# Down projection of channels 0 to 511 with tokens on the accumulators' partitions, and the last block stored by token groups from two queues

## The chip, the cores and the metric

The kernel runs on one core of a Trainium2 chip. The core has five engines with instruction streams of their own: TensorE (PE) multiplies matrices and writes only to PSUM, VectorE (DVE) and ScalarE (ACT) work element by element and read and write PSUM and SBUF, GpSimd (POOL) works on SBUF, and SyncE (SP) issues transfers between the chip's memory and SBUF. ACT can issue transfers too. A weight load (PEld) puts the stationary operand of a product into the array, 128 rows by up to 128 columns; then the other operand, 128 rows by up to 512 columns, moves through. The product has the stationary operand's columns on its partitions. The metric is the device time of one launch in microseconds (us), as the median of several runs.

## What is computed

One transformer-like block for 2048 tokens with 640 channels. A conditioning vector `c` gives six rows of 640 (`sa, ca, ga, sb, cb, gb`). The first half is a layer norm and a long convolution over the tokens (by Fourier transforms); the second half, where the change lies, is a gated feed-forward layer:

```python
h = _layernorm(x) * (1 + cb) + sb
gate = einsum("bsd,df->bsf", h, w1)      # 640 -> 1728
up   = einsum("bsd,df->bsf", h, w3)      # 640 -> 1728
out  = einsum("bsf,fd->bsd", silu(gate) * up, w2)   # 1728 -> 640, the down projection
x = x + gb * out
```

## The kernel before

**Tiling.** The 2048 tokens are four blocks (b = 0 to 3) of 512. In `x2[b]` a block lies with 128 tokens on the partitions, four token groups j beside each other and 640 channels each, so `x2[b][p, j, d]`. The hidden width 1728 is cut into 14 tiles m: thirteen of 128 and one (m = 13) of 64, which is stacked twice to fill 128 rows. The 640 channels of the output are five groups k of 128.

**Precision.** Every operand is split into a high and a low part (`split`, L595: ACT copies the high part, DVE subtracts for the low one), and a product is made of three: high by high, high by low, low by high.

**The passes.** `ffn` (L1344) runs two passes, p = 0 for blocks 0 and 1, p = 1 for blocks 2 and 3. In a pass, `groups` (L1355) goes through the hidden tiles and makes gate and up for both blocks by a seven-product scheme (`group`, L828, and `last_group`, L882); the hidden values of the first block of the pair go straight into the down projection (`mid`, L1366, calls `down` for the tile before), those of the second block are kept in SBUF as `h`. Then `late` (L1387) finishes the first block's accumulators, adds them to `x2` and stores them, while the down projection of the second block runs over the 14 kept tiles in the order `H` (13, 0, 1, ..., 12). In `late(0)` the layer norm of blocks 2 and 3 is interleaved as well, and after the loop `plain` makes tile 13 of blocks 2 and 3 (the `gh` products) before the second pass begins.

**The down projection.** `down` (L964) adds tile m to the five accumulators `acc[k]`, one PSUM bank of 512 columns each: channels on the partitions, the block's 512 tokens on the columns. A slice of w2 of 128 channels is stationary and the hidden values (`ah`, `al`) move. Per tile these are 15 products (10 for m = 13, whose low part lies in the stacked rows).

**Out of the accumulators.** `gated` (L974) copies `acc[k]` to SBUF on ACT and scales it by the gate of its channel, which is a number for each partition (`cols[:, 2, k]`). `output` (L979) turns the 128 x 512 tile back with four PE transposes into one bank, and DVE adds the bank to channels k of `x2[b]`. `store` (L987) writes `x2[b]` to the output, one transfer for each quarter q of the partitions.

**Banks and buffers.** Five of the eight PSUM banks are the accumulators; the other three rotate under the tag `gu` for everything else: the products of gate and up, the transposes of `output`, and those of the layer norm. w2 tiles rotate through three SBUF buffers (tag `w2`, 640 KB each); in `late`, tile i + 2 is asked for in iteration i (L1444), into the buffer that tile i - 1 leaves.

**Order.** PE's instructions in this part follow the order of the program text (the wrapper `InOrder`, L142, through which `self.pe` is called; its line L151 is the one that the profile names). The streams of the other engines and of SP are laid out in a fixed order before the launch; each engine then works through its own in order and waits on semaphores. In `late`, the list `extra` says after which iteration which piece of other work is put: the outputs of k = 0 after iteration 0, k = 1 and 2 after 1, k = 3 and 4 after 2, and the stores of the quarters after 3, 5, 7 and 9. The second block's last two tiles are kept back in `late(1)` (`LAST = 2`) and done group by group (L1451 to L1461), so that group k can be scaled, turned, added and stored while group k + 1 is multiplied: channels 0 to 383 in four transfers after k = 3, the remaining 256 channels in four more, two from SP and two from ACT.

Of the kernel before, what the change touches and what calls it, by code (L numbers as in the profile page):

```python
# [10 lines left out]
F32 = mybir.dt.float32  # L11
F32R = mybir.dt.float32r
I32 = mybir.dt.int32
AF = mybir.ActivationFunctionType
# [4 lines left out]
P = 128  # L19
L = 2048  # L20
D = 640
KT = D // P
# [183 lines left out]
class K:  # L206
# [757 lines left out]
    def down(self, acc, m, a, w, start, stop, ks=range(KT)):  # L964

        (ah, al), (w2h, w2l) = a, w
        for k in ks:
            sl = slice(k * P, (k + 1) * P)
            self.pe.matmul(acc[k], w2h[:, sl], ah, start=start, stop=False)
            self.pe.matmul(acc[k], w2l[:, sl], ah, start=False, stop=stop and m == 13)  # L970
            if m < 13:
                self.pe.matmul(acc[k], w2h[:, sl], al, start=False, stop=stop)

    def gated(self, b, acc, k):  # L974
        oc = self.tmp(f"oc{b}{k}")
        self.nc.scalar.activation(oc, acc[k], AF.Identity, scale=self.cols[:, 2, k:k + 1])
        return oc

    def output(self, b, oc, k):  # L979

        pt = self.bank(f"to{b}{k}")
        for j in range(4):
            self.pe.transpose(pt[:, j * P:(j + 1) * P], oc[:, j * P:(j + 1) * P], self.ident)
        xs = self.x2[b][:, :, k * P:(k + 1) * P]
        self.nc.vector.tensor_add(xs, pt.rearrange("p (j d) -> p j d", j=4), xs)

    def store(self, b, d0=0, d1=D, qs=range(4), other=None):  # L987
        for q in qs:
# [366 lines left out]
    def groups(self, p, tiles, X, acc, W, w2, pend):  # L1355

        for m in tiles:
            more = m < 12
            if more:
                raw = self.up_load(p, m + 1)  # L1360
                w2r = self.w2_get(2, m + 1) if p else self.w2_load(m + 1)
                sums, part, W2, _ = self.factors(p, m + 1, raw)
                sums()
            rows = []

            def mid():  # L1366
                if pend is not None:
                    self.down(acc, *pend, False)
                if p == 0 and m < 10:
                    rows.append(self.inverse_row(6 + m))  # L1370
                    rows[0](0)

            def quick():
                if rows:
                    rows[0](320)
            a = self.group(p, m, W, X, part, mid, quick) if more else self.last_group(p, m, W, X, mid)
            pend = (m, a, w2, False)
            if more:
                W, w2 = W2, w2r if p else self.w2_make(m + 1, w2r)
            if p == 0 and m in (8, 10):  # L1380
                b = m // 2 - 2
                self.stats[b % 2] = self.ln_stats(b, *self.ln_begin(self.fp, f"n{b}"), 0)
        return pend
# [3 lines left out]
    def late(self, p, acc, pend):  # L1387

        nc = self.nc
        b = 2 * p + 1  # L1390
        n = len(self.H)
        w2 = {i: self.w2_get(b, self.H[i]) for i in range(2)}
        X, v, xn = {}, {}, {}

        def hidden(i):
            return self.hidden_split(b, self.H[i], self.h.pop(self.H[i]), nc.vector)
        a = hidden(0)
        self.down(acc, *pend, True)
        oc = [self.gated(2 * p, acc, k) for k in range(KT)]
        acc = self.accumulators(b)  # L1400

        def norm(t):
            xn[t] = [self.norm(2 + t, j, *self.stats[t], "DVE" if j == 0 else "ACT") for j in range(4)]

        def turned(t, k):
            v[t, k] = self.tmp(f"v{2 + t}{k}") if t == 0 else self.tmp(f"v{2 + t}{k}", "hb", 10)
            self.turn_x(2 + t, k, xn[t], X, v[t, k], self.bank(f"tp{2 + t}{k}"))
        extra = {}

        def at(i, f, *a):  # L1410
            extra.setdefault(i, []).append((f, a))
        for k in range(KT):
            at((k + 1) // 2, lambda k=k: self.output(2 * p, oc[k], k))
        for q in range(4):
            at(3 + 2 * q, self.store, 2 * p, 0, D, (q,))
        box = {}
        if p == 0:
            at(1, norm, 0)
            for k, i in zip((0, 2, 1, 3, 4), (2, 3, 3, 4, 4)):
                at(i, turned, 0, k)  # L1420
            at(4, norm, 1)
            for k, i in zip((0, 2, 1, 3, 4), (6, 6, 7, 7, 8)):
                at(i, turned, 1, k)
            for c in range(2):
                at(8 + 2 * c, lambda c=c: self.x_sums(X, [v[0, c], v[1, c], v[0, 2 + c], v[1, 2 + c]], 1, c))

            def raws():
                box["half"] = self.whole(13, self.up_load(1, 13))

            def more():  # L1430
                box["W"] = self.factors(1, 0, self.up_load(1, 0))
            at(4, raws)
            at(6, more)

            def weights():
                sums, part, _, _ = box["W"]
                sums(nc.vector)
                for j in (0, 1, 7, 4, 3):
                    part(j)
            at(11, weights)  # L1440
        last = n - 2 if p else n
        for i, m in enumerate(self.H[:last]):
            if i + 2 < n:
                w2[i + 2] = self.w2_get(b, self.H[i + 2])  # L1444
            nxt = hidden(i + 1) if i + 1 < last else None
            self.down(acc, m, a, w2.pop(i), i == 0, i == n - 1)
            a = nxt
            for f, args in extra.get(i, ()):
                f(*args)
        if p:  # L1450
            keep = [(self.H[i], hidden(i), w2.pop(i)) for i in range(last, n)]  # L1451
            for k in range(KT):
                for m, a, w in keep:
                    self.down(acc, m, a, w, False, m == self.H[-1], [k])
                if k:
                    self.output(b, oc, k - 1)
                oc = self.gated(b, acc, k)
                if k == 3:
                    self.store(b, 0, 3 * P)
            self.output(b, oc, KT - 1)  # L1460
            self.store(b, 3 * P, D, other=nc.scalar)  # L1461
            return None
        w13 = self.w2_get(2, 13)
        oc = [self.gated(1, acc, k) for k in range(KT)]
        a, = self.plain(2, X, [(13, box["half"])])
        self.output(1, oc[0], 0)
        self.output(1, oc[1], 1)
        self.plain(3, X, [(13, box["half"])])
        _, part, W, _ = box["W"]
        for j in (5, 2, 6):  # L1470
            part(j)
        for k in range(2, KT):
            self.output(1, oc[k], k)
        self.store(1)
        return self.accumulators(2), X, W, self.w2_get(2, 0), (13, a, w13, True)
# [641 lines left out]
```

## Time and profile before

| | us |
|---|---|
| median of 3 runs | 946.92 |
| range of the runs | 946.81 to 948.67 |
| the profiled execution, whole | 947.64 |
| its span from first to last instruction | 945.9 |

Times in the profile count from the span's start. Roughly, the convolution fills the time to 400 us, the first pass 400 to 610, `late(0)` 610 to 680, the second pass 680 to 882, and `late(1)` the rest. Three views are used. A page sums up the whole execution: busy time of each engine, the chain of work that ended last followed back from the end, and groups of instructions (`L151 PE MATMUL acc<-ah,w` is a product at line 151 that reads `ah` and `w` and writes `acc`; then shapes, count, busy time in us and mean duration of one in ns). The timeline lists instructions in order: start, duration, engine, line, operation, output from inputs, and in brackets how long the engine had been idle and what ended that. `to` are the transposes of `output`, `oc` the copies of `gated`, `late` the SBUF tile that holds `x2[1]`, and `x` the tiles of the other `x2`. Windows give for a stretch of time how long each engine was busy, then the granted clock of PE (1.00 is full), the share of the 16 DMA engines' time and GB/s. Matmuls overlap: the duration of one is longer than the distance between the starts of two.

### The profile page before, as it was taken

The page shows a single profiled execution, that of the slowest core. Times are in us where ns is not written, and L with a number is a line of the kernel's source. Part 1 is how long each engine was busy: PE and PEld are TensorE (multiplying, and loading weights), DVE is VectorE, ACT ScalarE, POOL GpSimd, SP SyncE. Part 2 cuts the span into 40 slices and gives each one's busy share as a digit, 9 for nine tenths or more (in the row PEclk, how much of TensorE's full clock was granted, in tenths as well). Part 3 has the DMA queues.
Part 4 walks back from the last instruction along what each step waited for, and adds up shares of the span by engine and source line. Part 5 has one row for each costly group of instructions (what it writes and reads, how often), then busy time and mean ns, then how long its engine had stood idle before and what let it go on. Part 6 is the DMA issues. An engine that isn't in the chain of part 4 may idle for free.

```text
span 945.9 us, 21217 instructions
## 1 busy us (share of the span) xinstructions
PE 865.6 (92%) x8369; PEld 687.5 (73%) x8369; DVE 683.9 (72%) x1294; ACT 542.9 (57%) x1035; POOL 341.5 (36%) x370
## 2 busy tenths in 40 slices
PE   1267999999999997999999999999999999999997
PEld 1035857877888863787777778888788888888775
DVE  7997999999889978896776775657556555555412
ACT  6788999989787741754444444545444444443312
POOL 0899989998998500011111211000121212120000
PEclk9987999999999997999999999999999999999999
DMA  9876563525143598655433412375432222221374
GB/s 207 262 235 163 158 158 102 136 81 128 47 109 94 135 248 212 169 178 153 155 111 124 140 62 93 94 239 170 128 94 84 84 84 84 84 84 42 109 223 127
DMA packets 110508, 127.42 MB, mean 135 GB/s; under 512 B 10568, under 2 KB 90696, under 8 KB 109128
## 3 DMA queue, kind: packets, MB, share of 16 engines
q1 hardware_dynamic: 109032, 125.27, 46.3%
q8 instruction: 66, 1.08, 0.5%
q10 hardware_dynamic: 1376, 0.79, 0.3%
q14 instruction: 34, 0.28, 0.1%
HBM read 95.89 MB, written 30.15 MB: 133 GB/s over the span
## 4 chain that ended last, share of the span: by engine, by line
PE 74%; DVE 8%; ACT 7%; DMA 4%; POOL 2%; issue 2%; SPq 1%; ACTq 0%; DVEq 0%; POOLq 0%
PE c L151 19%; PE acc L151 18%; PE X L151 12%; PE ps L151 5%; PE fz L151 4%; PE gu L151 3%; PE kps L151 3%; PE fk L151 3%; PE fh L151 3%; DVE xb L151 1%; PE iy L151 1%; DVE yy L151 1%; ACT tr L151 1%; DMA zd<-zt 1%; PE tp L151 1%
## 5 line engine op out<-in xcount | busy, mean ns | idle before, releaser
L151 PE MATMUL acc<-ah,w 128*128 128x512 f32 x560 | 172.1, 393 | 2.6 <-DMA w<-w2d 1.9
L151 PEld LDWEIGHTS acc<-ah,w 128*128 128x128 f32 x560 | 103.6, 188 | 25.1 <-issue 2.3
L151 PE MATMUL acc<-al,w 128*128 128x512 f32 x260 | 101.4, 390 | 0.0
L151 ACT ACTIVATE tr<-ph 128x512 f32<-128x512 int32 (+1 forms) x160 | 93.7, 599 | 6.8 <-DVE yy L151 3.6
L597 DVE TENSOR_TENSOR wl<-s,wh 128x256 fp32r<-128x256 f32 x92 | 39.1, 425 | 65.8 <-ACT wh L596 65.5
L773 POOL TENSOR_TENSOR s<-wr 128x256 f32<-128x256 f32 x22 | 16.2, 737 | 181.8 <-DVE wl L597 103.5
L596 ACT ACTIVATE wh<-s 128x256 fp32r<-128x256 f32 x92 | 37.6, 410 | 77.0 <-PE X L151 57.1
L151 POOL TENSOR_TENSOR ph<-p,p 128x1024 int32<-128x1024 int32 x40 | 78.7, 1968 | 6.5 <-ACT tr L151 6.0
L596 ACT ACTIVATE wh<-wr 128x256 fp32r<-128x256 f32 x92 | 38.3, 418 | 54.8 <-PE X L151 41.9
L774 POOL TENSOR_TENSOR s<-s,wr 128x256 f32<-128x256 f32 x22 | 17.0, 772 | 131.8 <-issue 131.7
L151 DVE TENSOR_TENSOR yy<-yy,tr 128x512 f32<-128x512 f32 (+1 forms) x60 | 56.6, 945 | 3.2 <-ACT tr L151 2.2
L834 ACT ACTIVATE t<-g 128x512 f32<-128x512 f32 x44 | 27.8, 632 | 53.1 <-DVE g L798 53.1
L151 PEld LDWEIGHTS acc<-al,w 128*128 128x128 f32 x260 | 48.8, 188 | 10.7 <-DVE al L597 0.4
L803 DVE SCALAR_TENSOR_TENSOR g<-t,g 128x512 f32<-128x512 f32 x48 | 33.7, 702 | 31.3 <-ACT t L834 29.4
L151 DVE TENSOR_TENSOR xx<-tr,xx 128x512 f32<-128x512 f32 x80 | 54.2, 682 | 2.8 <-ACT tr L151 2.4
L151 PE MATMUL kps<-yy,xx 128*32 128x64 f32 x1920 | 38.6, 234 | 18.8 <-DVE xx L151 13.3
L151 PE MATMUL fz<-fp,wz 64*128 64x512 f32 x224 | 54.1, 608 | 0.4 <-DVE fp L151 0.4
L151 PEld LDWEIGHTS kps<-yy,xx 128*32 128x32 f32 x1920 | 33.4, 116 | 27.5 <-issue 12.3
L597 DVE TENSOR_TENSOR wl<-wr,wh 128x256 fp32r<-128x256 f32 x92 | 40.6, 442 | 14.4 <-ACT wh L596 14.3
L151 PE MATMUL ps<-wk,xb 128*64 128x128 f32 x640 | 47.4, 295 | 2.5 <-DVE hb L151 0.9
L151 PEld LDWEIGHTS ps<-wk,xb 128*64 128x64 f32 x640 | 43.3, 220 | 4.8 <-DVE hb L151 1.2
L596 ACT ACTIVATE ah<-h 128x512 fp32r<-128x512 f32 x26 | 16.4, 632 | 52.8 <-PE acc L151 52.8
(452 smaller groups left out, 2397.8 us busy)
## 6 DMA issues: line engine op xcount, KB each, us to landing
w<-w2d SPq DMA_DIRECT2D x42, 640.0 KB, 3.9
wr<-in_w SPq DMA_DIRECT2D x50, 320.0 KB, 3.7
zd<-zt SPq DMA_DIRECT2D x40, 256.0 KB, 3.2
w2d<-w SPq DMA_DIRECT2D x14, 640.0 KB, 3.4
xs<-in_x SPq DMA_DIRECT2D x16, 320.0 KB, 11.7
hs<-hb SPq DMA_DIRECT2D x20, 256.0 KB, 3.3
xb<-hs SPq DMA_DIRECT2D x20, 256.0 KB, 4.7
iz<-zd SPq DMA_DIRECT2D x32, 160.0 KB, 3.9
```

The costliest lines, as they stand in the source:

```text
L151: self.prev = self.k.order(f(*a, **kw), self.prev)
L596: self.nc.scalar.activation(H, v, AF.Copy)
L597: eng.tensor_tensor(Lo, v, H.bitcast(F32), op=ALU.subtract)
L773: eng.tensor_tensor(s[0], u[:, 0:2], u[:, 2:4], op=ALU.add)
L774: eng.tensor_tensor(s[1], s[0], g[:, 0:2], op=ALU.subtract)
L803: V.scalar_tensor_tensor(g, th, 1.0, g, op0=ALU.add, op1=ALU.mult)
L834: tanh = lambda o, i: A.activation(o, i, AF.Tanh, scale=0.5)
```

## The change

For k = 0 to 3 an accumulator now holds the token group k of the block on its partitions and channels 0 to 511 on its columns: a 128-token slab of the hidden values is stationary and 512 channels of w2 move. `acc[4]` stays as it was, with channels 512 to 639 on the partitions and 512 tokens on the columns. Thus only `acc[4]` needs transposes in `output`. The gate of channels 0 to 511 is needed along the columns now: `gate_row` makes it once, at the last tile of the first pass (m = 12, after the `down` in `mid`), by four transposes of a broadcast column into one `gu` bank and a copy on ACT into a buffer of the tag `w2r`, whose last load has been used by then.

For blocks 0 to 2, `gated` copies `acc[k]` without scaling for k < 4, DVE multiplies the copy by the gate row, and DVE adds it to token group k of `x2[b]` (`token_add`). In block 3 DVE multiplies straight out of PSUM; the groups run in the order 4, 0, 1, 2, 3, the transposed output of group 4 is put after the products of group 0, and each token group is stored by itself in four transfers of 80 KB (`store_row`), quarters 0 and 2 from SP, 1 and 3 from ACT.

```diff
     def down(self, acc, m, a, w, start, stop, ks=range(KT)):
         (ah, al), (w2h, w2l) = a, w
+        wide, rest = slice(0, 4 * P), slice(4 * P, D)
         for k in ks:
             sl = slice(k * P, (k + 1) * P)
-            self.pe.matmul(acc[k], w2h[:, sl], ah, start=start, stop=False)
-            self.pe.matmul(acc[k], w2l[:, sl], ah, start=False, stop=stop and m == 13)
-            if m < 13:
-                self.pe.matmul(acc[k], w2h[:, sl], al, start=False, stop=stop)
+            terms = [(ah, w2h), (ah, w2l), (al, w2h)][:3 if m < 13 else 2]
+            for i, (x, y) in enumerate(terms):
+                last = stop and i == len(terms) - 1
+                if k < 4:
+                    self.pe.matmul(acc[k], x[:, sl], y[:, wide], start=start and i == 0, stop=last)
+                else:
+                    self.pe.matmul(acc[k], y[:, rest], x, start=start and i == 0, stop=last)
+
+    def gate_row(self):
+        pt = self.bank("gb")
+        for k in range(4):
+            self.pe.transpose(pt[:, k * P:(k + 1) * P], bc(self.cols[:, 2, k], 1, P), self.ident)
+        self.gbrow = self.wp.tile([P, D], F32, name="gbrow", tag="w2r", bufs=2)[:, :4 * P]
+        self.nc.scalar.activation(self.gbrow, pt, AF.Copy)
 
     def gated(self, b, acc, k):
         oc = self.tmp(f"oc{b}{k}")
-        self.nc.scalar.activation(oc, acc[k], AF.Identity, scale=self.cols[:, 2, k:k + 1])
+        if k < 4:
+            self.nc.scalar.activation(oc, acc[k], AF.Copy)
+        else:
+            self.nc.scalar.activation(oc, acc[k], AF.Identity, scale=self.cols[:, 2, k:k + 1])
         return oc
 
     def output(self, b, oc, k):
+        if k < 4:
+            self.nc.vector.tensor_mul(oc, oc, self.gbrow)
+            self.token_add(b, oc, k)
+            return
         pt = self.bank(f"to{b}{k}")
...
+
+    def token_add(self, b, oc, k):
+        xs = self.x2[b][:, k, :4 * P]
+        self.nc.vector.tensor_add(xs, oc, xs)
+
+    def store_row(self, b, j):
+        for q in range(4):
+            (self.nc.scalar if q % 2 else self.nc.sync).dma_start(self.ov[q, :, b * 4 + j, :], self.x2[b][q * 32:(q + 1) * 32, j, :])
...
             def mid():
                 if pend is not None:
                     self.down(acc, *pend, False)
+                if p == 0 and m == 12:
+                    self.gate_row()
...
             keep = [(self.H[i], hidden(i), w2.pop(i)) for i in range(last, n)]
-            for k in range(KT):
+            for k in (4, 0, 1, 2, 3):
                 for m, a, w in keep:
                     self.down(acc, m, a, w, False, m == self.H[-1], [k])
-                if k:
-                    self.output(b, oc, k - 1)
-                oc = self.gated(b, acc, k)
-                if k == 3:
-                    self.store(b, 0, 3 * P)
-            self.output(b, oc, KT - 1)
-            self.store(b, 3 * P, D, other=nc.scalar)
+                if k == 4:
+                    oc = self.gated(b, acc, k)
+                    continue
+                if k == 0:
+                    self.output(b, oc, 4)
+                t = self.tmp(f"oc{b}{k}")
+                nc.vector.tensor_mul(t, acc[k], self.gbrow)
+                self.token_add(b, t, k)
+                self.store_row(b, k)
             return None
```

## Prediction

> **What bounds the kernel now.** I read the page first: the busy shares, the slices over time and the chain that ended last. A chip time is compared here with another to about 0.2% (1.9 us); less than that counts as no change.
>
> ```profile
> PE 865.6 (92%) x8369; PEld 687.5 (73%) x8369; DVE 683.9 (72%) x1294; ACT 542.9 (57%) x1035; POOL 341.5 (36%) x370
> ...
> PE 74%; DVE 8%; ACT 7%; DMA 4%; POOL 2%; issue 2%; SPq 1%; ACTq 0%; DVEq 0%; POOLq 0%
> ...
> L151 PE MATMUL acc<-ah,w 128*128 128x512 f32 x560 | 172.1, 393 | 2.6 <-DMA w<-w2d 1.9
> ...
> L151 PE MATMUL acc<-al,w 128*128 128x512 f32 x260 | 101.4, 390 | 0.0
> ...
> L151 PE MATMUL c<-x5h,wh 128*128 128x512 f32 x48 | 19.9, 414 | 0.1
> ```
>
> The first figure behind a name is busy time, the last before the bar's second part is the mean of one instruction. PE leads by busy time and by chain. The down projection is 820 products into `acc`. An average can hide the stage, so I then read the busy time stage by stage, and the chain in order of time.
>
> ```profile
> 700.00:840.00 140.00, 140.00 (x620) 115.95 (x619) 78.95 (x152) 60.68 (x135) 26.47 (x36) 1.00 0.28 85
> ...
> 698.64 3.40 PE acc L151 x15
> ```
>
> The columns after the window's length are the busy time of PE, weight loads, DVE, ACT and POOL. From 700 to 840 PE is busy all 140 us at full clock, DVE for 79. So a us taken out of PE's stream is a us gained, unless something else is then late. One product takes 3.40/15 = 0.227 us from start to start; the 390 ns of the page overlap.
>
> **The change part by part.** *Products.* As many as before, of the same shape: 4/5 of 820 = 656 now have a 128-token slab as the stationary operand and 512 channels of w2 moving. No row of before has a slab of tokens as weights for 128x512; the product rows above lie at 390 to 414 ns with quite different operands. I take 0 us.
>
> *Transposes.* Sixteen of the 20 outputs (four channel groups in four blocks) lose their four transposes, 64 in all, and the gate row adds four.
>
> ```profile
> L151 PE MATMUL to<-ident,oc x80: 270/272/328, 616.4 to 939.9; 128*128 128x128 f32 x80
> ...
> 620.03 0.40 PE L151 MATMUL acc<-al,w 128*128 128x512 f32 x1
> 620.27 1.04 PE L151 MATMUL to<-ident,oc 128*128 128x128 f32 x8
> 621.06 0.71 PE L151 MATMUL acc<-ah,w 128*128 128x512 f32 x2
> 621.61 0.39 PE L151 MATMUL acc<-al,w 128*128 128x512 f32 x1
> ```
>
> From 620.03 to 621.61 stand three products and eight transposes in 1.58 us; the products alone are worth 3 x 0.227 = 0.68, so eight transposes cost 0.90 and a set of four 0.45. Block 0 and block 2, whose outputs lie between products, lose four sets each: 1.8 us each. The gate row is a set of four among the last groups of the first pass, which are built like those of 700 to 840: +0.45. Its copy on ACT hides in ACT's free time (busy 60.68 of those 140 us); without that cover it would cost about 0.7, like a copy of `oc` (664.89 below, 3.41/5). Those copies lose their scale and stay one pass over the same tile: 0.
>
> *DVE.* Each of the twelve outputs of blocks 0 to 2 gets one multiply more, and its add reads SBUF instead of PSUM.
>
> ```profile
> 613.03 0.69 DVE L806 TENSOR_TENSOR h<-g,u 128x512 f32<-128x512 f32 x1
> ...
> 890.00:900.00 10.00, 10.00 (x54) 8.46 (x53) 3.80 (x7) 1.26 (x2) 0.00 (x0) 1.00 0.60 201
> ```
>
> A product of two SBUF tiles takes 0.69 us, like the adds out of PSUM (671.44 and 940.17 below), so 12 x 0.69 = 8.3 us of DVE come on top. In block 2 DVE is busy 3.8 of 10 us; a split (`al`) may be late by one or two such operations, and it is made a whole 3.4 us product group ahead. Cost 0; without that cover each late split would cost up to 0.7.
>
> *Block 1*, at the end of the first pass, stands differently: there PE waits.
>
> ```profile
> 664.89 3.41 ACT L976 ACTIVATE oc<-acc,cols 128x512 f32<-128x512 f32 x5 [3.67 <-PE acc L151]
> ...
> 667.57 3.40 PE gh L151 x15
> ...
> 671.44 1.29 DVE L985 TENSOR_TENSOR late<-to,late 128x512 f32<-128x512 f32 x2 [9.51 <-PE to L151]
> ...
> 672.19 0.50 PE L151 MATMUL gh<-x4h,wh_u 128*128 128x512 f32 x1 [0.35 <-DVE late L985]
> ...
> 677.46 0.66 PE L151 MATMUL to<-ident,oc 128*128 128x128 f32 x4 [0.69 <-DVE late L985]
> ...
> 678.48 0.50 PE L151 MATMUL X<-x0h,wh 128*128 128x512 f32 x1 [0.37 <-DVE late L985]
> ...
> 680.42 0.50 PE L151 MATMUL c<-x1h,wh 128*128 128x512 f32 x1 [0.27 <-DVE late L985]
> ...
> 681.12 0.69 DVE L954 TENSOR_TENSOR h<-h,gh 64x512 f32<-64x512 f32 x1
> ```
>
> PE waits for banks (three of them rotate) that the adds free one by one. From the chain's first gh product, 667.57, to `c` at 680.42 are 12.9 us. Needed there afterwards: 36 products (8.2) and one set of transposes (0.45), 8.6 us, so at most 4.3 are won. DVE has been idle for 9.5 us before 671.44, with `oc` ready from 665.6 on, so the eight multiplies and adds fit there (8 x 0.69 = 5.5). What is late next is the bank for `c`: that of the one remaining transposed output, freed by its add, or that of the second gh product, freed by the multiply that now ends at 681.8 and would end near 678.1 (its product is 0.9 earlier for two sets, and four adds, 2.8, no longer stand before it). The first gives 4.3, the second 2.3. I take 3.6, nearer to the first, since the row of 680.42 already shows `c` taking the bank of an add.
>
> *Block 2's store* shares its queue (SP) and the DMA engines with the w2 loads.
>
> ```profile
> 896.27 1.03 PE L151 MATMUL to<-ident,oc 128*128 128x128 f32 x8
> ...
> 896.46 0.32 SPq L745 DMA_DIRECT2D w<-w2d  x1
> ...
> 898.11 0.68 DVE L985 TENSOR_TENSOR x<-to,x 128x512 f32<-128x512 f32 x1
> ...
> 898.82 3.78 SPq L989 DMA_DIRECT2D out<-x  x4
> ...
> 903.01 24.03 SPq L745 DMA_DIRECT2D w<-w2d  x8
> ...
> 909.43 0.70 PE L151 MATMUL acc<-ah,w 128*128 128x512 f32 x2 [1.91 <-DMA w<-w2d]
> ...
> w<-w2d SPq DMA_DIRECT2D x42, 640.0 KB, 3.9
> ```
>
> The store of 1.3 MB goes out at 898.82, the next load behind it at 903.01, and PE waits 1.9 us for it. If only PE became faster, this wait would eat the 1.8 us. But the store waits for the last add, and that for the transposes after the third tile. These start 1.35 us earlier (three sets less) at 894.9 and are four instead of eight; with 0.6 for them and 0.7 for the add the store leaves at 896.3, 2.5 us earlier. The load before it (896.46 now, 3.9 to land) leaves only 1.35 earlier and still moves then. So the store's data, and the load behind them, gain between 1.35 and 2.5; I take 1.8: the wait stays at 2 us and block 2 keeps its 1.8. The ends are 0 (the load does not move) and 2.5. In block 0 the same order shows no wait; I take the whole 1.8.
>
> *The end.*
>
> ```profile
> 938.06 4.18 SPq L989 DMA_DIRECT2D out<-x  x6
> ...
> 938.30 0.39 PE L151 MATMUL acc<-al,w 128*128 128x512 f32 x1
> ...
> 940.17 0.69 DVE L985 TENSOR_TENSOR x<-to,x 128x512 f32<-128x512 f32 x1 [0.30 <-PE to L151]
> ...
> 940.89 1.38 ACTq L989 DMA_DIRECT2D out<-x  x2
> ...
> out<-x SPq DMA_DIRECT2D x4, 192.0 KB, 3.1
> ...
> out<-x ACTq DMA_DIRECT2D x2, 128.0 KB, 3.6
> ...
> 941.00:942.00 1.00, 0.00 (x0) 0.00 (x0) 0.00 (x0) 0.00 (x0) 0.00 (x0) 1.00 0.99 290
> ...
> DMA to landing us min/median/max: 2.4/3.4/5.8
> ...
> 944.00:945.00 1.00, 0.00 (x0) 0.00 (x0) 0.00 (x0) 0.00 (x0) 0.00 (x0) 0.50 0.31 105
> ```
>
> The first store waits until 938.06, so all 1.31 MB go at the end; the DMA engines (second last column) are full until about 944.3, and 1.6 us later the span ends. The store rows end in the median us from issue to landing. Afterwards two sets of transposes fewer stand before the last product: it starts at 938.30 - 0.90 = 937.4 and ends at 937.8. Multiply and add, one behind the other, take 1.4, and DVE is some 0.1 behind, for it has 1.4 per group like PE (6 x 0.227): 939.3. Three quarters of the output have left by then. The last row's four pieces are issued two by two on SP and ACT: 0.4 for the second, 3.1 to land, and 1.4 to the span's end (945.9 less 944.5, where ACT's pieces land, 3.6 after 940.89): 944.2. That is 1.7 us less; with the least landing 2.4 it is 2.4, with DVE two operations late 0.3.
>
> The store also goes from eight pieces to sixteen of 80 KB.
>
> ```profile
> xq<-in_x SPq DMA_DIRECT2D x4, 64.0 KB, 3.3
> ...
> 150.00:151.00 1.00, 0.91 (x18) 0.69 (x15) 1.00 (x3) 1.00 (x2) 1.00 (x2) 1.00 0.55 149
> ```
>
> Here 64 KB loads move at 149 GB/s. The first group's products end at 933.2 (937.8 less three groups of 1.36 and one set of 0.45); a multiply, two adds and some 0.7 to the first data make 936. Were 149 a limit, 1.31 MB would take 8.8 us, to 944.8, and 1.6 more: 946.4, so the end would lose 0.5 in place of winning 1.7. But the DMA engines are only 0.55 busy there, so the rate is that of one queue's issues, and here are two; I keep the 1.7.
> The Trainium skill, "DMA: Bandwidth & Descriptors", the table under Bandwidth, Measured, has 138 GB/s at 64 KB and asks for 1 MiB a transfer, which speaks against the change; the trace's 149 agrees in size. By the page's figure the end would lose 1.2, and the sum below would be 5.5 in place of 8.45.
>
> *Sum*: 1.8 + 3.6 + 1.8 + 1.7 - 0.45 = 8.45 us. The profiled execution had a span of 945.9 and took 947.64 in all; the median of the runs is 946.92. I take the sum from the median: 938.5 us.
>
> **The rivals.** *Block 1 keeps its waits* (`c` behind the second gh bank): 2.3 in place of 3.6, 939.8 us, and down to 1.8 (940.3) if more than the bank is late. For it: that bank's multiply is the last in DVE's queue now. Against it: the row of 680.42.
>
> *The store holds the load whatever PE does*: blocks 0 and 2 give back their 1.8 each, 942.1 us. For it is the 1.91 us wait, against it that the store's own release is an output of the shortened path.
>
> *Small stores are slow*, as the row of the 64 KB loads would have it: 2.2 less, 940.7 us. The Trainium skill's table named above would make it 941.4. A chance of 0.06 covers both.
>
> *Slower than before:* a product with a token slab as its weights is dearer, in the 656 places. From 8.45/656 = 13 ns each (0.240 in place of 0.227 us) nothing is won. The far bound is a start that no longer hides anything: after the transposes at 620.27 two products take 0.55 in place of 0.45 (621.06 to 621.61), and 0.10 in all 656 places would be 66 us, 1004 us. At 20 ns it is 13.1 - 8.45 = 4.7 slower, 951.6 us. For it speaks only that the trace has no such product; against it that rows with other operands agree within some ns.
>
> *More is won:* block 1 reaches 4.3, block 2 2.5, the end 2.4: 0.7 each, 10.6 us, 936.4.
>
> **How the numbers follow.** The forecast (937.2 to 939.5) gets 0.46; block 1 with its waits 0.18; the store holding the load 0.10; slow pieces 0.06; more won 0.11; dearer products 0.06; gain and loss even 0.03. So faster 0.91, same 0.03, slower 0.06. Two in ten may lie outside: the dear products, the even case, and the corners where several cases meet (940.3 with the store's loss would be 943.9; all far ends with less queueing than I counted, below 935.3). The range is 935.3 to 942.6; the likeliest case alone has 937.2 to 939.5.
>
> **What would show it.** `to` must fall from 80 transposes to 16, with four `gb` beside it, and the products stay at 820 with 3.40 us for 15. The waits for `late` between 672 and 681 must go, with `c` starting 3 to 4 us earlier there. DVE must show twelve multiplies more in blocks 0 to 2 without PE waiting for `al`. The wait for w2 in block 2 must stay near 2 us. The last add must end some 4.9 us before the span does, with idle DMA engines between the row stores. A product group of 3.5 us instead of 3.40, a longer wait for w2, or DMA engines full to the end would prove me wrong.

## The result and the profile after

The changed kernel takes 940.17 us, the median of 6 runs (939.97 to 943.16); the kernel before, run beside it, takes 947.23 (945.9 to 951.65). The ratio is 0.9924, with a 95% interval from 0.9906 to 0.9942: some 7 us faster, where 8.45 were forecast. The profiled execution took 940.2 us with a span of 938.4, against 945.9 before.

From the page of the changed kernel: busy time, the chain, and the groups of the products with tokens as weights (busy time and mean ns ahead of the second bar, PE's idle time ahead of them behind it).

```profile
PE 856.7 (91%) x8309; PEld 679.0 (72%) x8309; DVE 693.8 (74%) x1310; ACT 539.7 (58%) x1032; POOL 342.3 (36%) x370
...
PE 70%; DVE 12%; DMA 6%; ACT 5%; POOL 3%; issue 2%; SPq 1%; ACTq 0%; DVEq 0%; POOLq 0%
...
L151 PE MATMUL acc<-w,ah 128*128 128x512 f32 x448 | 137.0, 391 | 0.8 <-DMA w<-w2d 0.8
...
L151 PE MATMUL acc<-w,al 128*128 128x512 f32 x208 | 81.3, 391 | 2.0 <-DVE al L597 2.0
```

The 448 + 208 = 656 products with tokens as weights take 391 ns each, as the 390 and 393 of before: they are not dearer. What the change brought beside them is a new idle time of PE, 2.0 us for `al`. The view of PE's waits from 600 us on lists all that is left of it:

```profile
PE acc L151 <- DVE al L597: 2.0, 2, 1.3
PE c L151 <- DVE h L954: 1.6, 1, 1.6
PE acc L151 <- DMA w<-w2d: 0.8, 1, 0.8
PE c L151 <- DVE late L1004: 0.2, 1, 0.2
```

(Total, times, longest.) The waits for the adds into `late` are down to 0.2; in their place stand `al` and `h`, the second gh product's gate operation. The first of two timelines is that of the kernel before, at the seams between the stages:

```profile
610.00 0.61 PE L151 MATMUL acc<-ah,w 128*128 128x512 f32 x2
...
667.41 0.39 PE L151 MATMUL gh<-x0h,wh_u 128*128 128x512 f32 x1
...
683.97 0.84 PE L151 MATMUL acc<-ah,w 128*128 128x512 f32 x3
...
881.71 0.61 PE L151 MATMUL acc<-ah,w 128*128 128x512 f32 x2
```

The second is that of the changed kernel, with the waits:

```profile
600.31 0.39 PE L151 MATMUL acc<-al,w 128*128 128x512 f32 x1
600.54 0.60 PE L151 MATMUL gb<-ident,cols 128*128 128x128 f32 x4
600.89 0.48 PE L151 MATMUL X<-x3hT,wh 128*128 128x512 f32 x1
601.21 0.39 PE L151 MATMUL X<-x3lT,wh 128*128 128x512 f32 x1
...
610.23 0.62 PE L151 MATMUL acc<-w,ah 128*128 128x512 f32 x2
...
618.16 0.50 PE L151 MATMUL acc<-w,al 128*128 128x512 f32 x1 [1.27 <-DVE al L597]
...
667.04 0.39 PE L151 MATMUL gh<-x0h,wh_u 128*128 128x512 f32 x1
...
676.06 0.50 PE L151 MATMUL c<-x1h,wh 128*128 128x512 f32 x1 [0.21 <-DVE late L1004]
...
680.05 0.47 PE L151 MATMUL c<-x2hT,wh 128*128 128x512 f32 x1 [1.63 <-DVE h L954]
...
681.52 1.98 PE L151 MATMUL acc<-w,ah 128*128 128x512 f32 x8
...
879.25 0.62 PE L151 MATMUL acc<-w,ah 128*128 128x512 f32 x2
...
886.64 0.50 PE L151 MATMUL acc<-w,al 128*128 128x512 f32 x1 [0.75 <-DVE al L597]
...
904.80 0.70 PE L151 MATMUL acc<-w,ah 128*128 128x512 f32 x2 [0.84 <-DMA w<-w2d]
...
932.76 0.39 PE L151 MATMUL acc<-w,al 128*128 128x512 f32 x1
```

These seams divide the time into stretches that can be compared one by one. A is the first down product of the first pass's last group (610.00 and 610.23).

| stretch (us) | before | changed | difference |
|---|---|---|---|
| block 0: A to the first gh product | 57.41 | 56.81 | -0.60 |
| block 1: to the tile-13 products of the second pass | 16.56 | 14.48 | -2.08 |
| second pass, to its last group's down products | 197.74 | 197.73 | 0 |
| block 2: to the product that waits for w2, without the wait | 25.81 | 24.71 | -1.10 |
| that wait | 1.91 | 0.84 | -1.07 |
| the end: from there to the end of the span | 36.47 | 33.60 | -2.87 |
| A to the end | 335.90 | 328.17 | -7.73 |

Ahead of A lies the gate row: from 600.31 to 601.21 stand two products (0.45) and its four transposes, which leaves 0.45 for them. A lies only 0.23 later all the same: the down products of the tile ahead of the gate row started 0.24 earlier in this execution (597.14, before 597.38).

### The profile page after: what moved, and what is told of

Read it like the earlier page. It is cut to its first block, busy times and chain, and to the rows that moved or that the text cites. A ratio compares the mean times of both kernels' runs of the same rounds, so it can differ in the third digit from the quotient of the medians.

```text
span 938.4 us, 21120 instructions
## 1 busy us (share of the span) xinstructions
PE 856.7 (91%) x8309; PEld 679.0 (72%) x8309; DVE 693.8 (74%) x1310; ACT 539.7 (58%) x1032; POOL 342.3 (36%) x370
## 4 chain that ended last, share of the span: by engine, by line
PE 70%; DVE 12%; DMA 6%; ACT 5%; POOL 3%; issue 2%; SPq 1%; ACTq 0%; DVEq 0%; POOLq 0%
PE c L151 19%; PE acc L151 17%; PE X L151 12%; PE ps L151 5%; PE fz L151 4%; PE kps L151 3%; PE fk L151 3%; PE fh L151 3%; PE gu L151 2%; DMA zd<-zt 1%; DVE xb L151 1%; PE iy L151 1%; DVE yy L151 1%; DVE xx L151 1%; DMA sp<-zd 1%
## 5 line engine op out<-in xcount | busy, mean ns | idle before, releaser
L151 PE MATMUL acc<-w,ah 128*128 128x512 f32 x448 | 137.0, 391 | 0.8 <-DMA w<-w2d 0.8
L151 PEld LDWEIGHTS acc<-w,ah 128*128 128x128 f32 x448 | 83.4, 188 | 18.1 <-ACT ah L596 1.2
L597 DVE TENSOR_TENSOR wl<-s,wh 128x256 fp32r<-128x256 f32 x92 | 39.0, 424 | 65.3 <-ACT wh L596 65.0
L151 PE MATMUL acc<-w,al 128*128 128x512 f32 x208 | 81.3, 391 | 2.0 <-DVE al L597 2.0
L773 POOL TENSOR_TENSOR s<-wr 128x256 f32<-128x256 f32 x22 | 16.5, 748 | 179.2 <-DVE wl L597 111.2
L597 DVE TENSOR_TENSOR wl<-wr,wh 128x256 fp32r<-128x256 f32 x92 | 40.5, 441 | 14.4 <-ACT wh L596 14.3
L151 PEld LDWEIGHTS acc<-w,al 128*128 128x128 f32 x208 | 39.0, 188 | 11.1 <-DVE al L597 2.9
L775 POOL TENSOR_TENSOR s<-wr 128x256 f32<-128x256 f32 x22 | 16.9, 769 | 79.8 <-DVE wl L151 48.4
```

What stands on the lines that cost most here:

```text
L151: self.prev = self.k.order(f(*a, **kw), self.prev)
L597: eng.tensor_tensor(Lo, v, H.bitcast(F32), op=ALU.subtract)
L773: eng.tensor_tensor(s[0], u[:, 0:2], u[:, 2:4], op=ALU.add)
L775: eng.tensor_tensor(s[2], g[:, 0:2], u[:, 0:2], op=ALU.subtract)
```

## The experiments

A moves from 606.7 to 614.3 us among the runs, and not by the edits: these two are e4 and e5, whose edits lie behind A. So one time of one run tells little here: a run with a wait less can come out slower. Each run is therefore read in the same stretches from A on. Where nothing was edited, those of blocks 0 and 1 repeat within 0.04 us and the end behind the last product within some 0.3 us (5.57 to 5.91); the wait for w2 moves by more. The experiments are single runs but for e8. All edits are made in the changed kernel; the diffs show the lines that decide and leave out those that only note an instruction by a name such as `al_ins`.

| run | block 0 | block 1 | wait for w2 | last product to end | A to end |
|---|---|---|---|---|---|
| before | 57.41 | 16.56 | 1.91 | 7.60 | 335.90 |
| changed | 56.81 | 14.48 | 0.84 | 5.64 | 328.17 |
| e1 `al` first | 55.26 | 14.46 | 1.66 | 5.86 | 326.64 |
| e2 no multiply | 56.20 | 14.45 | 1.59 | 5.73 | 327.79 |
| e3 gh gate first | 56.80 | 13.74 | 1.71 | 5.72 | 328.46 |
| e4 store behind the loads | 56.80 | 14.48 | 0.98, elsewhere | 5.71 | 328.06 |
| e5 store by quarters | 56.80 | 14.45 | none | 5.62 | 327.03 |
| e6 rows emitted at the end | 56.81 | 14.48 | 1.58 | 5.57 | 328.88 |
| e7 block 3 alone | 57.40 | 16.56 | 2.30 | 5.91 | 335.33 |
| e9 block 3 alone, store by quarters | 57.42 | 16.58 | none | 5.89 | 331.14 |
| e10 rows behind the last | 56.81 | 14.47 | 1.55 | 9.01 | 332.29 |
| e11 one queue | 56.83 | 14.47 | 1.79 | 7.46 | 330.95 |
| e12 a fifth quarter | 56.80 | 14.47 | 3.16 | 5.71 | 332.17 |
| e8 four orders together | 55.25 | 12.88 | none | 5.86 | 323.13 |

### VectorE's order: e1, e2, e3

The theory after the result: the multiplies cost DVE little, but they stand in its queue ahead of the split that PE waits for.

e1 ties the multiplies behind the first `al`:

```diff
-            self.nc.vector.tensor_mul(oc, oc, self.gbrow)
+            self.order(self.nc.vector.tensor_mul(oc, oc, self.gbrow), self.al_ins)
```

> Only VectorE's order changes: in blocks 0 and 2 the first `al` of the kept tiles (at 617.42 and 885.90 in the changed kernel) is put ahead of the four gate multiplies. Theory (the multiplies are what makes TensorE wait): `acc<-w,al` no longer waits (1.27 + 0.75 = 2.0 us), the first gh product starts 0.9 to 1.3 us earlier (665.7 to 666.1 instead of 667.04), and the span falls by 1.5 to 2.0 us from 938.4, to 936.4 to 936.9. Rival 1 (`al` is late because its `ah` stands on ScalarE behind the four copies of the accumulators): both waits stay, span 938.4. Rival 2 (something else is late next, the norms and turns of blocks 2 and 3 among it): the waits go, and the first gh product stays within 0.3 us of 667.04.

e2 drops them, so that the gate of channels 0 to 511 is missing from blocks 0 to 2:

```diff
-            self.nc.vector.tensor_mul(oc, oc, self.gbrow)
             self.token_add(b, oc, k)
```

> The gate multiply of channels 0 to 511 is left out in blocks 0, 1 and 2 (12 VectorE instructions of 0.6 to 0.8 us); nothing else changes. Theory (their cost is the order, not the work): the same as with `al` moved ahead, waits of 2.0 us for `al` gone, span 936.4 to 936.9, and block 1 no faster than the changed kernel (wait of 1.63 us for the second gh product's bank within 0.3 us). Rival (VectorE's work itself bounds these stages): more is gained than by moving `al`, at least 1 us more, in block 1, where VectorE is busiest.

DVE's timeline of the changed kernel around the first wait:

```profile
613.26 0.69 DVE L806 TENSOR_TENSOR h<-g,u 128x512 f32<-128x512 f32 x1
613.87 3.03 DVE L997 TENSOR_TENSOR oc<-oc,gbrow 128x512 f32<-128x512 f32 x4
616.82 0.68 DVE L1008 TENSOR_TENSOR x<-oc,x 128x512 f32<-128x512 f32 x1
617.42 0.68 DVE L597 TENSOR_TENSOR al<-h,ah 128x512 fp32r<-128x512 f32 x1
```

and of e1:

```profile
614.40 0.69 DVE L806 TENSOR_TENSOR h<-g,u 128x512 f32<-128x512 f32 x1
616.22 0.86 DVE L597 TENSOR_TENSOR al<-h,ah 128x512 fp32r<-128x512 f32 x1 [1.12 <-ACT ah L596]
617.00 2.48 DVE L997 TENSOR_TENSOR oc<-oc,gbrow 128x512 f32<-128x512 f32 x4
```

Four multiplies and an add run ahead of `al`, which starts 4.16 us behind `h`; in e1 it starts 1.82 behind, as soon as its high part is there. Both waits for `al` are gone, and block 0 takes 1.55 us less. Block 2 without its wait for w2 takes 23.71 us in place of 24.71 (878.83 to 904.20, less 1.66). From A to the end only 1.53 of these 2.55 us show, as that wait was 0.82 longer than in the changed kernel's profile, which e4, e5 and e12 explain, and the end 0.22 longer; and the single time, 939.77 us (a span of 938.0, where 936.4 to 936.9 were expected), shows hardly anything, since A lay 1.1 us later too. In e2 the adds move up into the multiplies' place and `al` is still late by 0.69 us; block 0 wins 0.61. The expected end of both waits did not come, and the span of 936.4 us meets its figure only because A lay 1.6 us earlier. So leaving the work out brings less than putting it behind `al`: it is the order. Block 1 does not move in e2, so DVE's extra work does not bound it either.

e3 changes block 1's order:

```diff
-        a, = self.plain(2, X, [(13, box["half"])])
+        a = self.plain(2, X, [(13, box["half"])], False)
...
         self.plain(3, X, [(13, box["half"])])
+        a = self.hidden_split(2, 13, a, nc.vector)
+        self.order(self.sub_ins, self.gh_ins)
```

> Only block 1's order on VectorE changes: the split of block 2's tile 13 (L825, 1.12 us) is put behind the two gate operations of the second gh product (L953, L954), which free the bank that the first-pass-2 product at 680.05 waits for. Theory (the wait of 1.63 us is VectorE's queue ahead of L954): L954 ends some 1.1 us earlier, the wait falls to 0.3 to 0.7 us, the tile-13 products of block 1 start at 680.3 to 680.7 instead of 681.52, and the span falls by 0.8 to 1.3 us. Rival 1 (L953 waits for ScalarE's L952 or for POOL's sums beside it, not for L825): wait and span unchanged. Rival 2 (the split becomes late instead): the 1.63 us wait shrinks, and a wait of the same size for `ah` stands ahead of the tile-13 products.

DVE in the changed kernel ahead of the wait that ends at 680.05:

```profile
675.31 0.69 DVE L1004 TENSOR_TENSOR late<-to,late 128x512 f32<-128x512 f32 x1
675.92 0.51 DVE L597 TENSOR_TENSOR wl<-s,wh 128x256 fp32r<-128x256 f32 x1
676.46 1.12 DVE L825 TENSOR_TENSOR ah<-aa,t 64x512 fp32r<-64x512 f32 x1
677.50 1.23 DVE L953 SCALAR_TENSOR_TENSOR h<-th,h 64x512 f32<-64x512 f32 x1
678.76 0.42 DVE L597 TENSOR_TENSOR wl<-wr,wh 128x256 fp32r<-128x256 f32 x1
679.22 0.69 DVE L954 TENSOR_TENSOR h<-h,gh 64x512 f32<-64x512 f32 x1
```

From 675.31 DVE has no gap, and L954, which frees the bank, is the last in the row. With L825 behind it, the wait fell from 1.63 to 0.91 us and block 1 by 0.74; no wait for `ah` came up. The forecast was a wait of 0.3 to 0.7 us; the difference is that a weight split (L597, 0.85 us in that run) still stood between the two gate operations. e8 moves that one as well and wins 1.60, nearly all of the wait.

### The load behind the store: e4, e5, e12

e4 ties the four transfers of block 2's store behind the last load of w2, e5 puts one quarter each behind the loads for tiles 5, 7, 9 and 11, and e12 adds one more transfer of 320 KB to the four (the diff has e5 and e12):

```diff
 e5
-            at(3 + 2 * q, self.store, 2 * p, 0, D, (q,))
+            at(4 + 2 * q if p else 3 + 2 * q, self.store, 2 * p, 0, D, (q,))
...
+            if b == 2:
+                self.last_sp = self.order(ins, self.last_sp)
 e12
+            at(3, self.store, 2)
+            at(3, self.store, 0, 0, D, (0,))
```

> Block 2's store (4 x 320 KB) leaves SyncE's queue behind the last load of down weights (922.1) instead of ahead of the load at 898.43. Theory (the load that is late by 0.84 us at 904.80 is late by sharing the DMA engines with the store, 6.2 us to landing against 4.0 for the others): all loads land in about 4.0 us, the wait is 0, the span falls by 0.8 us, and the row stores of block 3 still land in 2.1 to 2.4 us since the moved store ends by about 928. Rival 1 (the load is late because its buffer comes free late, at 898.43): the wait stays 0.8. Rival 2 (the moved store meets the row stores): the 0.8 us is given back at the end, span 938.4 or more.

> Block 2's store is put into SyncE's queue one quarter (320 KB) at a time, behind the loads of down weights for tiles 5, 7, 9 and 11 of block 3's order, instead of four in a row ahead of one load. Theory (a load is late when the whole store stands ahead of it or lands with it; in the normal case its lead over its product is about 2.8 us longer than its 4.0 us to landing): every load lands within 5.5 us, TensorE waits for no down weights after 890 us (0.84 us in the changed kernel, 0.98 with the store behind the last load). Rival (a quarter, too, delays the next load past its product): one or more waits of 0.3 to 1 us remain.

> The changed kernel with one transfer more in SyncE's queue: behind the four quarters of block 2's store, and ahead of the next load of down weights, a quarter of block 0 (320 KB) is stored a second time with the values it has. Five of six runs with the four quarters there had a wait of 1.55 to 1.79 us for that load (the profile of the changed kernel 0.84). Theory on the wait (the load is late by what stands in the queue ahead of it): a quarter costs 0.8 to 1.2 us there, so 2.4 to 2.9 us. Rival: within 0.2 us of the 1.55 to 1.79. On the clock, theory: idle time of TensorE over some 2.0 to 2.3 us takes its granted clock to 0.5 for some 3 us behind it (at 2.30 it did, at 1.91 and 1.79 not), so the products from that wait to the last two tiles take 22.1 us in place of 20.5. Rival: the gap has to be longer, about 3.4 us, and the run with 2.30 had another cause; 20.5 us and a granted clock of 1.00.

In e4 the wait at that load went, and one of 0.98 us came up at the last load, which was sent off 0.4 us ahead of the store and took 4.90 us to land, 3.8 in the changed kernel: sharing the DMA engines is enough. From A to the end nothing was won (328.06 us). In e5 no load took longer than 4.6 us and no wait was left. In e12 the wait was 3.16 us, more than the 2.4 to 2.9 expected; the six runs that left this order alone (e1, e2, e3, e6, e10, e11) each had 1.55 to 1.79, so a fifth quarter cost the load about 1.5 us. The profiled execution of the changed kernel, with 0.84, was the lucky one; against the one 1.91 of before, some 0.8 of its 1.07 us there are not the change's doing.

### The end: e6, e10, e11

e6 puts all `store_row` calls behind the loop:

```diff
                 self.token_add(b, t, k)
-                self.store_row(b, k)
+            for k in range(4):
+                self.store_row(b, k)
```

> Block 3 is stored with the same 16 pieces of 80 KB from the same two queues, all of them behind the last addition. The measure is the stretch from the start of the last product to the end of the span: 5.64 us in the changed kernel (932.76 to 938.4), 7.60 in the kernel before (938.30 to 945.9). Theory (three of four rows land while TensorE still works): the stretch grows by the landing of 0.98 MB at the 225 to 300 GB/s at which the stores of the other blocks land, 3 to 4 us, to 8.6 to 9.8 us. Rival (the end is the fixed time of issue and landing, and the rows could have waited): within 0.4 us of 5.64.

5.57 us. But the edit moves nothing: the queues hold the same transfers in the same order, and each still waits for its own addition alone. The run says only how well this measure repeats. e10 therefore changes the order, so that all stand behind the last row:

```diff
-                self.store_row(b, k)
+            last = {}
+            for k in (3, 0, 1, 2):
+                self.store_row(b, k, last)
```

> Block 3's rows leave in the order 3, 0, 1, 2 on both queues, so that the three earlier rows stand behind the last one, which waits for the last addition: now all 1.31 MB leave behind it. The measure is from the start of the last product to the end of the span, 5.64 us in the changed kernel and 5.57 to 5.91 in the runs so far. Theory (three of four rows land under TensorE's work): 0.98 MB more at 225 to 300 GB/s, 3.3 to 4.4 us more, 8.9 to 10.2. Rival (issue and the landing of the last piece set the end): under 6.5.

9.01 us, as expected: leaving while PE still works is worth 3.4 us to the rows.

e11 sends all 16 pieces from SP:

```diff
-            (self.nc.scalar if q % 2 else self.nc.sync).dma_start(...)
+            self.nc.sync.dma_start(...)
```

> All 16 row pieces leave from SyncE's queue, none from ScalarE's. The measure is from the start of the last product to the end of the span, 5.57 to 5.91 us so far. Theory (a queue sends a piece of 80 KB off every 0.32 to 0.5 us, and the last row's four pieces are two deep on two queues, four deep on one): 0.6 to 1.0 us more, 6.2 to 6.9. Rival 1 (the second queue brings nothing, since the pieces share the DMA engines): within 0.2 us of 5.6 to 5.9. Rival 2 (one queue is held up by the earlier rows): 2 us or more.

7.46 us, 1.8 more than the changed kernel: above the theory's range, and just short of the 2 us of rival 2, whose cause it is, a queue held up by the earlier rows. A row of e11's timeline shows it, four pieces in SP's queue:

```profile
938.65 1.82 SPq L1012 DMA_DIRECT2D out<-x  x4
```

Four pieces, as many as a row has, take 1.82 us to send off, and a row is made in 1.36 (six products of 0.227). One queue falls 0.46 us further behind with each row; the last piece left at 940.52, 2.8 us behind the last addition (937.00 + 0.69), and the span ended 2.4 us after it had been sent off. With two queues a row takes half and there is no backlog.

### Does it add up: e7, e9

e7 puts blocks 0 to 2 back to channels on partitions; e9 has the quarters of e5 as well:

```diff
-                if k < 4:
+                if k < 4 and tok:
...
-            self.down(acc, m, a, w2.pop(i), i == 0, i == n - 1)
+            self.down(acc, m, a, w2.pop(i), i == 0, i == n - 1, tok=p == 1)
```

> Blocks 0, 1 and 2 go back to channels on partitions (transposes, gate as a scale on ScalarE); only block 3 has tokens on partitions, the gate row and the row stores. Since what comes ahead of the last group of the first pass differs by some us from run to run, the measure is the time from the first down product of that group to the end of the span: 335.9 us before (945.9 - 610.00), 328.2 changed (938.4 - 610.23). Theory (the four places add up: block 0 0.6, block 1 2.1, block 2 2.2, end 2.9): 335.9 - 2.9 = 333.0, and 57.4 and 16.6 us for the stretches of blocks 0 and 1 as before. Rival (the end's gain hangs on the earlier blocks' gains, as a later end of the loads would have it): 334.5 or more.

> The kernel with tokens on partitions in block 3 alone (blocks 0 to 2 as before), with block 2's store by quarters. In the run of the former the wait for down weights was 2.30 us, TensorE's granted clock then fell to 0.50 to 0.55 for some 3 us, and the products of block 3 took 1.62 us more than in the changed kernel (909.20 to 931.33 against 904.80 to 925.32). Theory (the dip comes of that wait): no wait for weights and no dip, from the first down product of the last group to the end 335.33 - 2.30 - 1.62 = 331.4 us, which with the wait of before (1.91) put back is 333.3, the sum of the kernel before less block 3's own gain (333.0). Rival (the dip is of the layout or of the chip, not of the wait): the wait goes, a dip remains, 333.0.

e7 came out at 335.33, as its rival had it, but not for the rival's reason. The products behind its wait ran slowly; these are windows of e7 (granted clock of PE third from the end):

```profile
906.90:909.20 2.30, 0.00 (x2) 0.03 (x1) 0.69 (x1) 0.44 (x1) 0.00 (x0) 1.00 0.99 385
909.20:910.20 1.00, 1.00 (x4) 0.82 (x5) 0.00 (x0) 0.00 (x0) 0.00 (x0) 0.85 0.98 404
910.20:912.20 2.00, 2.00 (x7) 1.52 (x6) 0.00 (x0) 0.00 (x0) 0.00 (x0) 0.50 0.18 74
912.20:914.20 2.00, 2.00 (x8) 1.62 (x7) 0.00 (x0) 0.00 (x0) 0.00 (x0) 0.72 0.00 0
914.20:917.00 2.80, 2.80 (x14) 2.31 (x13) 0.69 (x1) 0.63 (x1) 0.00 (x0) 1.00 0.48 177
```

The clock is down to a half for some 3 us, and the products from there to the last two tiles took 22.13 us (909.20 to 931.33) in place of 20.52. e9, the same layout without the wait, has no dip and takes 331.14. Against the kernel before without its wait (335.90 - 1.91 = 333.99) block 3 by itself thus wins 2.85 us, the 2.87 of the first table. So the end's gain adds to that of the other three places and does not hang on them; those three were not tried one by one.

### The four orders together: e8

e8 joins e1, e3 and e5 and moves the weight split of e3 behind the bank as well:

```diff
             W[i] = self.operand(i, f"{p}{m}", src[i], V)
+            if (p, m, i) == (1, 1, 0):
+                self.order(self.low_ins, self.gh_ins)
```

> Four orders together: `al` ahead of the gate multiplies in blocks 0 and 2; the gate operations of the second gh product ahead of block 2's tile-13 split; the first split of tile 1's weights in the second pass behind them as well; block 2's store by quarters. Nothing is computed otherwise. Theory (the changed kernel's four late waits, 2.0 for `al`, 1.6 for the second gh product's bank, 0.8 to 1.7 for the weights, are all VectorE's and SyncE's order): all of them fall below 0.4 us in sum 0.6 at most, from the first down product of the last group to the end 328.2 - 1.5 - 1.4 - 0.75 - 0.84 = 323.7 (323.2 to 324.5), and the timed kernel is 3.5 to 5 us faster than the changed kernel, ratio to the kernel before 0.986 to 0.989. Rival (what is freed is taken by the next wait): 326 or more for that stretch, ratio 0.991 or more.

934.02 us, the median of 6 runs (932.8 to 936.39), against 947.0 (944.32 to 952.94, 11 runs) for the kernel before: a ratio of 0.9859, interval 0.9829 to 0.9889, which does not meet that of the change alone. From A to the end it takes 323.13 us, a little under the 323.2 to 324.5 expected. PE's waits behind 600 us, where the changed kernel had four rows:

```profile
PE c L151 <- DVE late L1009: 0.2, 1, 0.2
```

## Why the prediction was right, and where it was not

The time, 938.5 us, was 1.7 below the measured one, and the sum of 8.45 stands against 7.28 in the profile (7.73 less the gate row's 0.45). Behind that lie five terms off by about a microsecond each, which cancel in part: -1.2 (block 0), -1.5 (block 1), -0.7 (block 2), +1.1 (the wait for w2, of which some 0.8 is luck), +1.2 (the end). The 940.17 us lie in the range (935.3 to 942.6) but outside the likeliest case (937.2 to 939.5); they are nearer to the rival in which block 1 keeps its waits (939.8 to 940.3).

**Products, transposes, gate row: right.** 391 ns in the new form; the second pass has not moved (197.73 us). `to` fell from 80 to 16, and the gate row cost its 0.45. The rival of dearer products falls with this.

**DVE at no cost: wrong, and this is the step that failed.** "A split (`al`) may be late by one or two such operations, and it is made a whole 3.4 us product group ahead." The first `al` behind the accumulators is not made ahead. Its high part comes from ACT behind four copies of accumulators, and PE needs `al` at the third product of the group. The cover was read from the middle of block 2 (890 to 900), not from the stage's start; and not one or two operations stood ahead of it but five. The waits were 1.27 and 0.75 us, and block 0 won 0.60 and block 2 1.10 in place of 1.8 each. e1 and e2 showed it.

**Block 1: the right bank for `c`, and one bank too few.** From the first gh product, `c` came 4.0 us earlier (from 13.01 to 9.02 behind it), so it did take the bank of an add. But the two candidates were taken as alternatives. They come one after the other: the product behind `c` takes the second gh product's bank, and that was free only at 679.9, where 678.1 had been counted. L825 and two weight splits stood ahead of it, and L825 and L953 took 1.12 and 1.23 us, not 0.69. So 2.08 came of 3.6, near the rival with 2.3. e3 got 0.74 of the rest back, and e8 all of it (12.88 us, 3.68 less than before).

**The store and the load: right.** The store did leave earlier as PE did, and the wait stayed: 1.55 to 1.79 in six runs of the same order against 1.91. The 0.84 of the one profile is scatter. The rival in which the store holds the load whatever PE does is refuted.

**The end: right in its parts but one.** The last product starts 0.91 us earlier behind the wait for w2 (28.87 to 27.96), as counted, but the landing was mis-sized, as the transfers of the changed kernel show (size of one, median us from issue to landing):

```profile
out<-x SPq DMA_DIRECT2D x8, 80.0 KB, 2.1
out<-x ACTq DMA_DIRECT2D x8, 80.0 KB, 2.4
```

2.1 and 2.4 us where 3.1 had been taken from a transfer of 192 KB, although those of 128 KB took 3.6. The last add, the last row of DVE's timeline, ends 3.8 us ahead of the span's end (934.61 to 938.4), not 4.9:

```profile
933.92 0.69 DVE L1008 TENSOR_TENSOR x<-oc,x 128x512 f32<-128x512 f32 x1
```

Of these 1.1 us the landing explains 0.7, since the last row's pieces took 2.4; most of the rest is the time behind the last landing, some 0.9 us in place of 1.4. And the DMA engines are not idle between the rows, as a window of the changed kernel shows (their share is second from the end):

```profile
934.00:935.00 1.00, 0.00 (x0) 0.00 (x0) 0.61 (x1) 0.00 (x0) 0.00 (x0) 1.00 0.79 210
```

**Small stores** are not slow. Even on one queue (e11) 1.31 MB go out in the 7.3 us of the issues, 179 GB/s, and what limits is the sending off. The Trainium skill, "DMA: Bandwidth & Descriptors", the table under Bandwidth, Measured, has 138 GB/s at 64 KB, for loads issued from GpSimd; the stores here were not held to that.

## What to carry to other kernels

When work is added to an engine that has time to spare, look at its queue at the seam where the added instructions land: the question is which instruction stands behind them and who waits for it, not the busy share of the stage. When one of several rotating buffers comes free earlier, follow the next takers too, until one finds its buffer free anyway. And read an edit worth a microsecond in stretches of the trace between fixed instructions, since stages that it does not touch can move the whole time by more.

## What the hardware showed that was not expected

**A wait can cost more than its length.** A gap of 2.30 us (e7) was followed by some 3 us at half clock and cost 1.6 us more; one of 3.16 us (e12) was too, and its products up to the last two tiles took 22.12 us as well (908.02 to 930.14). These are windows of e12, from the gap's end on:

```profile
908.00:909.00 1.00, 0.98 (x3) 0.85 (x4) 0.00 (x0) 0.00 (x0) 0.00 (x0) 0.65 0.81 338
909.00:911.00 2.00, 2.00 (x6) 1.54 (x6) 0.00 (x0) 0.00 (x0) 0.00 (x0) 0.50 0.14 52
911.00:913.00 2.00, 2.00 (x9) 1.62 (x8) 0.00 (x0) 0.00 (x0) 0.00 (x0) 0.82 0.00 0
```

The 22.12 us are what e12 was expected to show, and after gaps of 1.91 us and less in these stages the clock stayed at 1.00. But the length of the gap alone does not decide. Near 348 us, in the convolution, PE waits once for ACT in nearly every run. In the kernel before and in e10, which are alike up to there, this gap was 2.17 us long. The rows show the first products behind it and the window that follows, first of the kernel before, then of e10:

```profile
349.55 1.13 PE L151 MATMUL fh<-sp,wb 128*64 128x128 f32 x16 [2.17 <-ACT zt L151]
349.60:352.00 2.40, 2.40 (x34) 2.03 (x36) 0.36 (x2) 0.60 (x1) 0.00 (x0) 1.00 1.15 305
...
348.59 1.98 PE L151 MATMUL fh<-sp,wb 128*64 128x128 f32 x16 [2.17 <-ACT zt L151]
348.60:351.00 2.40, 2.40 (x23) 2.40 (x25) 0.12 (x1) 0.34 (x1) 0.00 (x0) 0.50 1.11 304
```

The clock stayed full in the one and was halved in the other; the changed kernel had 2.50 us there and kept 1.00. And behind the last product, where PE has nothing more to do, the clock fell after 2.4 us in e2 and e8, but not in the 5.2 us up to the end of the span in e6. So no single length separates the gaps that cost from those that do not. It seems to matter at which moment a gap falls; what sets that moment is not shown. The Trainium skill, "TensorE: Matmul & The Clock Gate", section "HAM oscillation — how this bites in real kernels", says: "The abstract rule is 'no PE-idle gaps >~3.4µs.'" The gaps of 2.17 us (e10), 2.30 (e7) and 3.16 (e12) were shorter and the clock was halved behind them, so staying under that figure was not enough here.

**VectorE was slower beside GpSimd.** Around the bank that came free late, GpSimd's timeline in the changed kernel has three sums:

```profile
675.41 0.73 POOL L774 TENSOR_TENSOR s<-s,wr 128x256 f32<-128x256 f32 x1 [59.66 <-issue]
676.23 0.80 POOL L776 TENSOR_TENSOR s<-wr,s 128x256 f32<-128x256 f32 x1
676.99 1.19 POOL L775 TENSOR_TENSOR s<-wr 128x256 f32<-128x256 f32 x1
```

L825 and L953, which ran on VectorE at 676.46 and 677.50 beside them, took 1.12 and 1.23 us. In e3 L825 ran at 679.20, behind the sums (the last ended at 678.27), and took 0.69. The Trainium skill, "SBUF — State Buffer", section "SBUF: two separate sides", says that a VectorE operation with two inputs in SBUF and a GpSimd operation that reads SBUF lock each other out for a whole instruction. These operations have two such inputs and were slower beside the sums, so far the rows agree. A lock for a whole instruction they do not show: L825 started 0.57 us ahead of the second sum's end (676.46 to 677.03) and took only 0.43 us longer. A run without the sums was not made.
